# A row spread over the partitions by TensorE instead of by two transfers, once, in a Fourier mixing and feed-forward kernel

## The chip, the cores and the metric

The kernel runs on one core of a Trainium2 chip. The metric is the device time of one execution in microseconds. The engines are called as in the profile: PE (TensorE, with PEld for its weight loads), DVE (VectorE), ACT (ScalarE), POOL (GpSimd) and SP (SyncE, which here only issues transfers).

## The reference

For each of 8 batches of 3008 x 256 numbers, a Fourier transform runs along the sequence and then along the 256 features, and the real part is kept. Its 24064 rows then go through a feed-forward layer of 2048 inner features with the gate h * cos(h):

```python
X = np.fft.fft(x, axis=1)
X = np.fft.fft(X, axis=2)
x = X.real.reshape(24064, 256)
h = x @ w_in
g = h * np.cos(h)
out = g @ w_out
```

All of it is in 32-bit floats.

## The kernel before, in words

The transform along the sequence has two halves. `first_half` multiplies folded pieces of x by a small matrix (47 points), the result is rearranged by way of DRAM (`store_z`, `load_z`), and `second_half` multiplies by the 64-point part with the twiddle factors. The feature transform is folded into `w_in`, which gives two weight tiles `WC` and `WS`.

The outputs of one batch are worked through in 6 groups of columns (225 columns in group 0, 256 in the others). `second_half(b, g)` makes what a group needs: four pairs of matmuls into a borrowed PSUM bank `pb`, an ACT copy (L377) into the tile `pq`, and the tile `nb`. The second half of row 0 of `pq` holds the values of the Nyquist feature, and `nb` is this row repeated on all 128 partitions. For nearly all groups SP does that with two transfers, one of the row to a small DRAM tile `nd` (L383), and one back with a broadcast (L384). Only for the very first group, `spread_nb` does it otherwise: a matmul with a row of ones as weights (L391) writes the repeated row into a PSUM bank, and ACT copies it to `nb` (L392).

A group has 8 steps of two half-steps each; half-step k works on 128 of the 2048 inner features. The main loop runs over k (t is k // 2), and everything in it is written out by hand: the order of the program is the order on every engine, and nothing is planned by a scheduler. Several half-steps overlap. For one half-step the work is:

- ACT writes the seed, 0.25 plus a weight times `nb`, into a PSUM bank H (`seed`, L525). This is done one half-step ahead.
- PE adds the products with `WC` (`mm1(.., 0)`, L544), ACT keeps twice that in `ew` (`act_e`, L556), PE adds the products with `WS` (`mm1(.., 1)`, L544), and DVE writes the mirrored side (`dve_h`, L560).
- ACT rounds (L572), DVE takes the fraction (L576), ACT takes the sine (L582), and DVE forms the product with h (`dve_g`, L586), the last reader of the bank H.
- Once per step POOL forms sums of the products into a tile `S` (`sums`, L602, L608, L609), and PE multiplies seven blocks by combinations of `w_out` (`mm2`, L635), five half-steps behind (`LAG`).

The four H banks go round in turn. `borrow` gives the bank whose turn is next without moving the turn; what is written there must be read before the next seed writes it. At the end of each odd half-step come the combinations of finished groups, the stores of output (`store_out`), and the calls that the table `opening` names for step t (only in the first batch), then those that `transform` has set for the next batch: its loads of x (`load_x`, L147 to L155, on SP), its folds (`fold`, L241, on POOL), its halves of the transform. In step 4 the table calls `second_half(0, 1)`, and the calls for the next batch in the same step add `load_x(1, 2)`. Group 1 starts with half-step 16; its first seed is issued at the end of half-step 15. `combine_w2` in the same table forms combinations of `w_out` on POOL (L510) in steps 0 to 6.

```python
        4: ((combine_w2, 4, 6, 2, 4), (second_half, 0, 1)),
        5: ((combine_w2, 6, 8, 0, 2),),
```

SP takes its transfers strictly in the order of the program, and each is issued once its waits are over: the data, the room, and mostly the landing of the transfer issued eight before it, since eight semaphores go round.

Of the kernel before, what the change touches and what calls it, by code (L numbers as in the profile page):

```python
# [82 lines left out]
def _width(g):  # L83
    return 225 if g == 0 else 256
# [24 lines left out]
def kernel(  # L109
# [100 lines left out]
    def psum(name, tag="H"):  # L210
        at = tag
        if tag == "H":
            at = f"H{turn[0] % 4}"
            turn[0] += 1
        return ppool.tile([128, 512], FP, tag=at, bufs=bank[tag], name=name)

    def borrow(name, k=0):
        return ppool.tile([128, 512], FP, tag=f"H{(turn[0] + k) % 4}", bufs=1, name=name)
# [132 lines left out]
    ready = {}  # L351

    def second_half(b, g):

        T = _width(g)
        z2 = z2s[b]
        pb = borrow("pb") if b or g else psum("pb", "M")
        for q in range(4):
            jj = 4 * g + q
            nc.tensor.matmul(  # L360
                pb[:, 128 * q : 128 * q + 128],
                lhsT=z2[:, jj * 128 : jj * 128 + 128],
                rhs=BJ[:, jj * 128 : jj * 128 + 128],
                start=q == 0,
                stop=True,
                skip_group_check=True,
            )
        pq = spool.tile([128, 512], FP, tag="pq", bufs=8, name="pq")
        pv = pq[:, 0 : 2 * T].rearrange("d (e t) -> d e t", e=2)
        bv = pb.rearrange("d (q e k) -> d e q k", q=4, e=2)  # L370
        if g == 0:
            nc.scalar.copy(
                out=pv[:, :, 0:192].rearrange("d e (q k) -> d e q k", k=64), in_=bv[:, :, 1:4, :]
            )
            nc.scalar.copy(out=pv[:, :, 192:225], in_=bv[:, :, 0, 0:33])
        else:
            nc.scalar.copy(out=pv.rearrange("d e (q k) -> d e q k", k=64), in_=bv)  # L377
        nb = spool.tile([128, 256], FP, tag="nb", bufs=8, name="nb")
        ready[b, g] = (pq, nb)
        if b == 0 and g == 0:  # L380
            return
        nd = dpool.tile([1, 256], FP, tag="nd", bufs=4, name="nd")
        nc.sync.dma_start(out=nd[:, 0:T], in_=pq[0:1, T : 2 * T])  # L383
        nc.sync.dma_start(out=nb[:, 0:T], in_=nd[0:1, 0:T].to_broadcast([128, T]))  # L384


    def spread_nb():
        pq, nb = ready[0, 0]
        T = _width(0)
        pn = psum("pn", "M")  # L390
        nc.tensor.matmul(pn[:, 0:T], lhsT=ones, rhs=pq[0:1, T : 2 * T], start=True, stop=True)  # L391
        nc.scalar.copy(out=nb[:, 0:T], in_=pn[:, 0:T])  # L392

# [4 lines left out]
    def transform(b):  # L398
        todo = {}

        def at(o, *call):
            todo.setdefault(o, []).append(call)

        for p in range(4):
            at(2 * p, load_x, b, p)
            at(7 + p, take_middle, b, p)
            for k in range(4):
                at(8 * p + (6, 7, 9, 10)[k], fold, b, 2 * p + k // 2, k % 2)
            pairs[per * (b - 1) + 8 * p + 12] = b, 2 * p
            for c in (2 * p, 2 * p + 1):  # L410
                at(8 * p + 12, store_z, b, c)
        middles.add(per * (b - 1) + 11)
        at(23, load_z, b, 0)
        at(39, load_z, b, 1)
        for g in range(NG):
            at(42 + g, second_half, b, g)
        return todo
# [111 lines left out]
    def seed_first(h):  # L529
        s, T = h.s, h.s.T  # L530
        nc.tensor.matmul(
            h.H[:, 0:T],
            lhsT=wrow[:, 128 * h.u : 128 * h.u + 128],
            rhs=s.pq[0:1, T : 2 * T],
            start=False,
            stop=True,
            skip_group_check=True,
        )

    def mm1(h, e):  # L540
        s, T = h.s, h.s.T
        W = WS if e else WC
        f = 2 * s.fp + h.u
        nc.tensor.matmul(  # L544
            h.H[:, 0:T],
            lhsT=W[:, 128 * f : 128 * f + 128],
            rhs=s.pq[:, e * T : e * T + T],
            start=False,
            stop=True,
            skip_group_check=True,  # L550
        )

    def act_e(h):
        T = h.s.T
        h.ew = spool.tile([128, 256], FP, tag="ew", bufs=2, name="ew")
        nc.scalar.mul(out=h.ew[:, 0:T], in_=h.H[:, 0:T], mul=2.0)  # L556
# [27 lines left out]
    def dve_g(h):  # L584
        r, y = sides(h)
        nc.vector.scalar_tensor_tensor(  # L586
            out=r, in0=y, scalar=-0.25, in1=r, op0=ALU.add, op1=ALU.mult
        )
# [236 lines left out]
    for half in range(2):  # L825
# [5 lines left out]
        0: ((combine_w2, 0, 2), (combine_w2, 2, 4)),  # L831
        3: ((combine_w2, 4, 6, 0, 2),),
        4: ((combine_w2, 4, 6, 2, 4), (second_half, 0, 1)),
        5: ((combine_w2, 6, 8, 0, 2),),
        6: ((combine_w2, 6, 8, 2, 4),),
        10: ((second_half, 0, 2), (load_ident,)),
        14: ((second_half, 0, 3),),
# [12 lines left out]
    def step(t, last=None):  # L850
        s = steps[t] if 0 <= t < n else None
        return s if s is not None and (last is None or s.fp == 7) else None
# [3 lines left out]
    def unit(k):  # L856
        return halves[k] if 0 <= k < 2 * n else None
# [7 lines left out]
    for k in range(2 * n + LAG):  # L865
        t, u = divmod(k, 2)
        d, v = divmod(k - LAG, 2)
        cur, prev, old, nxt = unit(k), unit(k - 1), unit(k - 2), unit(k + 1)
        done = step(d)
        full = step(d if v else d - 1, True)  # L870
        if cur:
            if k % (2 * per) == 0:
                todo = transform(cur.s.b + 1) if cur.s.b + 1 < NB else {}
            if k >= AHEAD:
                mm1(cur, 0)
                act_e(cur)
            if k == 0:
                for h in (cur, nxt):
                    mm1(h, 0)
                    seed_first(h)  # L880
                    act_e(h)
                spread_nb()
            if k < AHEAD - 1:
                mm1(cur, 1)
            if k == 0:
                pw = [weights(1, 3)]
        pair = None if u else pairs.pop(t, None)
        if pair:
            b, c = pair
            pz = [first_half(b, c, borrow("pz"))]  # L890
        if old:
            dve_g(old)
            if old.u:
                sums(old.s)
        if pair:
            pz.append(first_half(b, c + 1, borrow("pz", 1)))
        pm = clear_middle() if u and t in middles else None
        if done:
            order = (0, 1, 5, 4, 3, 2, 6) if done is steps[-1] else range(7)
            mm2(done, 4 * v, 4 * v + 3, order)  # L900
        if pm is not None:
            middle(pm)
        if full and full is not steps[-1]:
            take_m(full, 1 if v else 3, nc.vector)
        if nxt and 0 < k < AHEAD - 1:
            seed(nxt)
        if prev:
            act_round(prev)
        if pm is not None:
            nc.scalar.copy(out=zm[64:128], in_=pm)  # L910
        if pair:
            keep_z(b, c, pz[0])
        if nxt and k >= AHEAD - 1:
            seed(nxt)
        if full and full is not steps[-1]:
            take_m(full, 0 if v else 2, nc.scalar)
        if prev:
            dve_frac(prev)
        if k + 1 in range(2, AHEAD):
            mm1(nxt, 0)  # L920
            act_e(nxt)
        if k == 1:
            pw.append(weights(0, 3))
        copy_small()
        if prev:
            act_sin(prev)
        if pair:
            keep_z(b, c + 1, pz[1])
            patch_z(b, c)
            patch_z(b, c + 1)  # L930
        if cur and k >= AHEAD - 1:
            mm1(cur, 1)
        if done and v == 0:
            mm2(done, 3, 4, order)
        if cur:
            dve_h(cur)
        if k in (1, 2):
            keep_weights(2 - k, 3, pw[k - 1], nc.vector.tensor_copy)
        elif k == 3:
            send_wn(3)  # L940
        elif k == 6:
            load_wn(3, nc.scalar)
        if u == 0:
            continue
        for i in range(6):
            s = step(t - 4 - i, True)
            if s:
                combine_m(s, i)
        for sg, lag in ((0, 8), (1, 10)):
            s = step(t - lag, True)  # L950
            if s:
                store_out(s, sg)
        for call in opening.pop(t, ()):
            call[0](*call[1:])
        for call in todo.pop(t % per, ()):
            call[0](*call[1:])
# [31 lines left out]
```

## Time and profile before

| | us |
|---|---|
| median of 3 runs | 1954.21 |
| lowest and highest run | 1953.16, 1957.72 |
| the profiled execution | 1952.79 |
| its span | 1951.0 |
| PE busy | 1935.9 (99%) |
| DVE, ACT, POOL busy | 1457.7, 1508.9, 1400.2 |
| mean granted clock of PE | 0.999 of full speed |

The span runs from the first to the last instruction that the profiler recorded, and the execution's own time has 1.8 us more around it. A matmul in 32-bit floats shows as two pieces of PE work. A line of the timeline gives the start, the time, the engine, the line of the kernel, the operation with its tiles, and in brackets how long the engine stood idle before it and on what. A line of the stretches gives, after the stretch and its length, for PE, PEld, DVE, ACT and POOL the busy time with the number of instructions, then the granted clock, the share of the transfer engines and the GB/s.

### The profile page before, as it was taken

The page shows a single profiled execution, that of the slowest core. Times are in us where ns is not written, and L with a number is a line of the kernel's source. Part 1 is how long each engine was busy: PE and PEld are TensorE (multiplying, and loading weights), DVE is VectorE, ACT ScalarE, POOL GpSimd, SP SyncE. Part 2 cuts the span into 40 slices and gives each one's busy share as a digit, 9 for nine tenths or more (in the row PEclk, how much of TensorE's full clock was granted, in tenths as well). Part 3 has the DMA queues.
Part 4 walks back from the last instruction along what each step waited for, and adds up shares of the span by engine and source line. Part 5 has one row for each costly group of instructions (what it writes and reads, how often), then busy time and mean ns, then how long its engine had stood idle before and what let it go on. Part 6 is the DMA issues. An engine that isn't in the chain of part 4 may idle for free.

```text
span 1951.0 us, 29624 instructions
## 1 busy us (share of the span) xinstructions
PE 1935.9 (99%) x9232; PEld 1682.9 (86%) x9232; DVE 1457.7 (75%) x2531; ACT 1508.9 (77%) x3444; POOL 1400.2 (72%) x1594
## 2 busy tenths in 40 slices
PE   8999999999999999999999999999999999999998
PEld 4888899888988889888898888988889888898887
DVE  3667777777777777777777777777777777778787
ACT  3777778777787777877778787787777887778775
POOL 3777767787677876787668776687767777666765
PEclk9999999999999999999999999999999999999999
DMA  7712024111230112301241111411124121110001
GB/s 184 141 27 44 20 47 84 24 36 33 53 71 18 40 40 59 54 20 40 43 78 31 32 34 41 86 24 39 24 42 84 24 40 28 39 22 16 11 14 31
DMA packets 178280, 88.71 MB, mean 45 GB/s; under 512 B 104890, under 2 KB 175209, under 8 KB 176492
## 3 DMA queue, kind: packets, MB, share of 16 engines
q1 hardware_dynamic: 176582, 86.35, 21.7%
q8 instruction: 75, 1.23, 0.3%
q14 instruction: 81, 0.66, 0.1%
q10 hardware_dynamic: 1542, 0.47, 0.1%
HBM read 49.51 MB, written 37.28 MB: 44 GB/s over the span
## 4 chain that ended last, share of the span: by engine, by line
PE 98%; DMA 1%; ACT 0%; DVE 0%; SPq 0%; issue 0%; POOL 0%; POOLq 0%; DVEq 0%
PE M L635 58%; PE H L544 33%; PE pz L269 3%; PE pb L360 2%; PE pw L427 1%; DMA xp<-in_x_dram 0%; DMA wr<-in_moe_w_in_dram 0%; DMA nb<-nd 0%; DMA nd<-pq 0%; PE pz L266 0%; PE pm L317 0%; DVE r L576 0%; DVE cb L703 0%; ACT r L582 0%; POOL xf L252 0%
## 5 line engine op out<-in xcount | busy, mean ns | idle before, releaser
L602 POOL TENSOR_TENSOR S<-r 128x512 f32<-128x512 f32 (+1 forms) x383 | 475.6, 1242 | 447.1 <-DVE r L586 398.5
L576 DVE SCALAR_TENSOR_TENSOR r<-r,H 128x512 f32<-128x512 f32 (+1 forms) x768 | 518.3, 675 | 195.5 <-ACT r L572 168.7
L582 ACT ACTIVATE r<-r 128x512 f32<-128x512 f32 (+1 forms) x768 | 477.0, 621 | 240.1 <-DVE r L576 235.2
L586 DVE SCALAR_TENSOR_TENSOR r<-H,r 128x512 f32<-128x512 f32 (+1 forms) x768 | 518.9, 676 | 133.8 <-ACT r L582 93.9
L635 PE MATMUL M<-S,VX 128*128 128x256 f32 (+1 forms) x2304 | 616.0, 376 | 0.0
L635 PEld LDWEIGHTS M<-S,VX 128*128 128x128 f32 x2304 | 436.0, 190 | 71.5 <-issue 22.7
L544 PE MATMUL H<-pq,WC 128*128 128x256 f32 (+1 forms) x1536 | 454.0, 377 | 3.9 <-ACT H L525 3.9
L544 PE MATMUL H<-pq,WS 128*128 128x256 f32 (+1 forms) x1536 | 451.1, 375 | 1.0 <-ACT ew L556 1.0
L572 ACT ACTIVATE r<-H 128x512 f32<-128x512 f32 (+1 forms) x768 | 447.7, 583 | 0.2 <-DVE H L560 0.2
L560 DVE TENSOR_TENSOR H<-ew,H 128x256 f32<-128x256 f32 (+1 forms) x768 | 324.7, 423 | 142.5 <-PE H L544 83.6
L635 PE MATMUL M<-r,w 128*128 128x256 f32 (+1 forms) x1536 | 387.6, 375 | 0.0
L556 ACT ACTIVATE ew<-H 128x256 f32<-128x256 f32 (+1 forms) x768 | 287.9, 375 | 121.5 <-PE H L544 117.0
L525 ACT ACTIVATE H<-nb,wn 128x256 f32<-128x256 f32 (+1 forms) x766 | 366.0, 478 | 4.9 <-DMA nb<-nd 4.0
L635 PEld LDWEIGHTS M<-r,w 128*128 128x128 f32 x1536 | 300.5, 196 | 26.9
L544 PEld LDWEIGHTS H<-pq,WC 128*128 128x128 f32 x1536 | 279.3, 190 | 48.3 <-ACT H L525 13.1
L544 PEld LDWEIGHTS H<-pq,WS 128*128 128x128 f32 x1536 | 290.0, 190 | 34.7 <-issue 1.6
L608 POOL TENSOR_TENSOR S<-S,r 128x256 f32<-128x256 f32 (+1 forms) x383 | 276.0, 721 | 30.0
L609 POOL TENSOR_TENSOR S<-r,S 128x256 f32<-128x256 f32 (+1 forms) x383 | 275.2, 718 | 30.0
L635 PE MATMUL M<-S,w 128*128 128x256 f32 (+1 forms) x768 | 225.5, 375 | 0.0
L635 PE MATMUL M<-r,VX 128*128 128x256 f32 (+1 forms) x768 | 225.2, 375 | 0.0
L635 PEld LDWEIGHTS M<-S,w 128*128 128x128 f32 x768 | 150.8, 197 | 14.6
L635 PEld LDWEIGHTS M<-r,VX 128*128 128x128 f32 x768 | 145.8, 190 | 14.6
(78 smaller groups left out, 918.1 us busy)
## 6 DMA issues: line engine op xcount, KB each, us to landing
out_dram<-ob SPq DMA_DIRECT2D x724, 32.0 KB
xp<-in_x_dram SPq DMA_DIRECT2D x56, 256.0 KB
zd<-zs SPq DMA_DIRECT2D x112, 96.0 KB
z<-zd SPq DMA_DIRECT2D x28, 384.0 KB
xp<-in_x_dram SPq DMA_DIRECT2D x56, 120.0 KB
nb<-nd SPq DMA_DIRECT2D x40, 128.0 KB
wr<-in_moe_w_in_dram SPq DMA_DIRECT2D x8, 256.0 KB
w<-in_moe_w_out_dram SPq DMA_DIRECT2D x4, 512.0 KB
```

What stands on the lines that cost most here:

```text
L525: nc.scalar.activation(out=h.H[:, 0:T], in_=s.nb[:, 0:T], func=AF.Copy, bias=0.25, scale=wn[:, f : f + 1])
L544: nc.tensor.matmul(h.H[:, 0:T], lhsT=W[:, 128 * f : 128 * f + 128], rhs=s.pq[:, e * T : e * T + T], start=False, stop=True, skip_group_che ...
L556: nc.scalar.mul(out=h.ew[:, 0:T], in_=h.H[:, 0:T], mul=2.0)
L560: nc.vector.tensor_tensor(out=h.H[:, T : 2 * T][:, ::-1], in0=h.ew[:, 0:T], in1=h.H[:, 0:T], op=ALU.subtract)
L572: nc.scalar.activation(out=r, in_=y, func=AF.Copy, bias=BIG, scale=1.0)
L576: nc.vector.scalar_tensor_tensor(out=r, in0=r, scalar=-BIG, in1=y, op0=ALU.add, op1=ALU.subtract)
L582: nc.scalar.activation(out=r, in_=r, func=AF.Sin, bias=0.0, scale=SIN_SCALE)
L586: nc.vector.scalar_tensor_tensor(out=r, in0=y, scalar=-0.25, in1=r, op0=ALU.add, op1=ALU.mult)
L602: tt(out=sv[:, 0:2], in0=qv[:, 1:2].to_broadcast([128, 2, T]), in1=qv[:, 0:4:3], op=ALU.subtract,)
L608: tt(out=sv[:, 2], in0=sv[:, 1], in1=gv[:, 0, 0], op=ALU.subtract)
L609: tt(out=sv[:, 3], in0=gv[:, 1, 0], in1=sv[:, 2], op=ALU.add)
L635: nc.tensor.matmul(acc[key][m // 2][:, 256 * (m % 2) : 256 * (m % 2) + T], lhsT=w, rhs=a, start=first, stop=s.fp == 7, skip_group_check=True,)
```

## The change

The row of group 1 of the first batch is spread in the same way as that of group 0. `second_half(0, 1)` stops before the two transfers. `spread_nb` takes the group as an argument, and for group 1 the matmul writes to a borrowed H bank instead of one of the banks for the outputs. It is called at the end of step 5, which is half-step 11, one step after `second_half(0, 1)`. All other spreads stay as they were.

```diff
-        if b == 0 and g == 0:
+        if b == 0 and g < 2:
             return
         nd = dpool.tile([1, 256], FP, tag="nd", bufs=4, name="nd")
         nc.sync.dma_start(out=nd[:, 0:T], in_=pq[0:1, T : 2 * T])
         nc.sync.dma_start(out=nb[:, 0:T], in_=nd[0:1, 0:T].to_broadcast([128, T]))
 
-    def spread_nb():
-        pq, nb = ready[0, 0]
-        T = _width(0)
-        pn = psum("pn", "M")
+    def spread_nb(g):
+        pq, nb = ready[0, g]
+        T = _width(g)
+        pn = borrow("pn") if g else psum("pn", "M")
         nc.tensor.matmul(pn[:, 0:T], lhsT=ones, rhs=pq[0:1, T : 2 * T], start=True, stop=True)
         nc.scalar.copy(out=nb[:, 0:T], in_=pn[:, 0:T])
...
-        5: ((combine_w2, 6, 8, 0, 2),),
+        5: ((combine_w2, 6, 8, 0, 2), (spread_nb, 1)),
...
-                spread_nb()
+                spread_nb(0)
```

## The prediction

> **What bounds the kernel now.** I read the page's busy times first, then the two-microsecond stretches around the place where PE pauses, then the list of waits, the timeline there, and SyncE's queue in the chain that ended last.
>
> Busy time by engine:
>
> ```profile
> PE 1935.9 (99%) x9232; PEld 1682.9 (86%) x9232; DVE 1457.7 (75%) x2531; ACT 1508.9 (77%) x3444; POOL 1400.2 (72%) x1594
> ```
>
> PE is idle for 15.1 us of 1951.0, so whatever the change gives must lie in those 15 us or in time when PE runs slowly. In the stretches after 82 us PE is busy in every microsecond up to 1930. The stretches in question (per engine the busy us, then granted clock, DMA share, GB/s):
>
> ```profile
> 70.00:72.00 2.00, 2.00 (x12) 1.89 (x10) 1.74 (x4) 1.22 (x3) 1.84 (x4) 1.00 0.13 37
> 72.00:74.00 2.00, 0.25 (x2) 0.00 (x0) 0.30 (x1) 0.00 (x0) 2.00 (x3) 1.00 0.65 113
> 74.00:76.00 2.00, 0.28 (x1) 0.28 (x2) 0.00 (x0) 0.81 (x2) 1.84 (x3) 0.86 1.08 182
> 76.00:78.00 2.00, 2.00 (x6) 1.71 (x7) 0.79 (x2) 1.19 (x4) 1.43 (x2) 0.50 1.12 181
> 78.00:80.00 2.00, 2.00 (x10) 1.82 (x9) 0.90 (x3) 0.98 (x5) 0.00 (x0) 0.79 1.01 137
> 80.00:82.00 2.00, 2.00 (x12) 1.92 (x11) 1.62 (x3) 1.61 (x4) 1.26 (x2) 1.00 1.07 120
> ```
>
> PE, DVE and ACT stand still from 72.25 to 75.2; then PE runs at a granted clock of 0.50 until about 78.9. The timeline names the cause:
>
> ```profile
> 71.33 0.54 PE L544 MATMUL H<-pq,WS 128*128 128x225 f32 x2
> 71.70 0.54 PE L635 MATMUL M<-S,VX 128*128 128x225 f32 x2
> ...
> 75.19 0.48 ACT L525 ACTIVATE H<-nb,wn 128x256 f32<-128x256 f32 x1 [3.97 <-DMA nb<-nd]
> ...
> 75.72 1.22 PE L544 MATMUL H<-pq,WC 128*128 128x256 f32 x2 [3.48 <-ACT H L525]
> ...
> 79.36 0.59 PE L544 MATMUL H<-pq,WC 128*128 128x256 f32 x2
> ...
> 81.74 0.59 PE L544 MATMUL H<-pq,WC 128*128 128x256 f32 x2
> ...
> 83.75 0.62 PE L544 MATMUL H<-pq,WC 128*128 128x256 f32 x2
> ```
>
> The seed of the first half-step of group 1 (half-step 16) needs nb of group 1. In SyncE's queue the copy to DRAM is issued at 68.11 and the copy back at 71.01:
>
> ```profile
> 67.55 0.41 SPq L155 DMA_DIRECT2D xp<-in_x_dram  x1
> 68.11 0.22 SPq L383 DMA_DIRECT2D nd<-pq  x1
> 71.01 0.36 SPq L384 DMA_DIRECT2D nb<-nd  x1
> 71.47 0.37 SPq L147 DMA_DIRECT2D xp<-in_x_dram  x1
> ```
>
> pq itself was written at 59.65 to 60.24. The chain that ended last gives the two transfers 2.89 and 4.16 us: nb lands at 75.17, and the seed starts at 75.19. So this round trip is on the path, once in the kernel.
>
> **The change, part by part.**
>
> *The wait that goes.* At 0.19 us a 225-column piece, the pair at 71.70 lets the next matmul start at 72.08. It starts at 75.72: 3.64 us. The half-step it opens then takes 75.72 to 79.36 = 3.64 us; the half-step of the same shapes two later takes 81.74 to 83.75 = 2.01 us. So 1.63 us are lost to the slow clock (from 75.72 to about 78.9 at half speed is 3.2 / 2 = 1.6, the same). Together 5.27 us.
>
> [...] The row: 0.86, 0.50 and 0.79 of three 2 us stretches make 0.28 + 1.00 + 0.42 = 1.70 us of clock lost, that is 3.4 us at half clock, after a pause of 3.5 us. [...]
>
> *Added on PE.* One matmul of a single row by 256 columns at the end of half-step 11, which in the trace of before is between the S,VX pair of 63.33 and the WC pair of 63.71. A pair of 256-column pieces takes 0.43 us start to start (78.92 to 79.36 is 0.44). Where single-row pieces stand between full ones, the starts are further apart: L544 at 36.80 to L531 at 37.38 is 0.58 instead of 0.38, and L391 at 37.86 to L544 at 38.33 is 0.47. Lower bound 0.43, upper 0.43 + 0.2 + 0.2 = 0.83; I take 0.7, nearer the rows that change from full to one row. PE is without a gap there (60 to 72 us), so all of it lands on the path. Its operands: pq has been there since 60.24; the borrowed bank was last read by the DVE product of half-step 9, at 62.23 to 62.85, 0.86 us before the matmul's turn. No wait on either.
>
> *Added on ACT.* One 128x256 copy out of the bank: the row for 128x225 is 0.35, for 128x512 (L377) 0.59, the 128x256 multiplication 0.38. I take 0.38. It stands behind the sine at 63.58 and ahead of the multiplication L556 at 64.29, which waits for WC of half-step 12. That WC is itself 0.7 later behind the new matmul, so the copy sits in the time ACT would wait: at 64.4 the pair for nb is done, copy to 64.8, WC done at 63.71 + 0.7 + 0.54 = 64.95. Cost on the path 0; if the cover is gone, at most 0.38. Queued behind the copy are the round and the seed of half-step 13 (64.97 to 65.43), which goes into this very bank; WC of 13 starts at 65.61, and both move by about the same 0.4 to 0.7.
>
> *Removed from SyncE.* Two issues (L383, L384), and the 3 us for which SyncE's queue stood at the second. Eight issues of x for batch 1 (71.47 to 75.19), of which the last started as nb landed, move up to about 68.1 to 71.5. Who needs them: the folds at 88.36 and 93.01 and the ACT copies at 88.37 and 93.59, none waiting for a transfer; they come 4.6 earlier, the loads about 3 earlier, and DMA is quiet (share 0.32 in 80 to 90). Gain or loss 0. The other 46 spreads keep their way and none makes ACT wait (only one wait on nb in the list).
>
> *What is late next.* POOL, which used the pause to catch up. It is busy 9.53 of 10 us from 60 to 70, and works without a gap to 77.43 (fold, sums of step 6 at 73.67 to 76.21, fold). Without the pause PE wants the first of these sums, ready at 74.73, by half-step 17's last S product, at 72.08 + 2.01 + 0.43 + 1.14 + 0.43 = 76.1, and the last, ready at 76.21, at about 77.7. Then step 7's sums run 77.43 to 80.0, wanted from 80.5. At least 1.4 us of slack everywhere, more with the new matmul in front. ACT: the seed of half-step 16 comes right after the round of 70.69, at 71.1 to 71.6, in time for 72.08. Cost 0.
>
> *Sum.* 5.27 - 0.7 = 4.6 us (4.4 to 4.8 by the bounds of the matmul alone). The profiled execution took 1952.79 us, span 1951.0 and 1.8 around it; it is 1.4 below the median 1954.21 of the runs. It would come to 1948.2, and I expect the median at 1954.21 - 4.6 = 1949.6.
>
> **The rivals.**
>
> *The slow clock is no part of the usual execution.* Then only 3.64 - 0.7 = 2.9 us are saved: 1951.3. [...] Against it: the runs are all above the profiled execution, while those without the slow clock should lie 1.6 below.
>
> *Another wait takes the place, on ACT.* ACT is busy 7.96 of 10 us in 60 to 70; if the copy and the longer chain behind it push the seeds 1 to 2 us out, PE pauses there and gets back part: gain 2.6 to 3.6, about 1951.2. For it: seeds already hold PE weight loads 43 times in the trace. Against it: 13.1 us in all, most of it this one pause, and the busy share leaves ACT 0.4 us in each half-step of 2.1 us.
>
> *Slower: POOL's sums of steps 6 and 7 come too late without the pause.* Place: the S products of half-steps 17 to 20. A PE pause of 3.0 us with the clock loss of 1.6 behind it uses up the 4.6; with the 1.4 us of slack, it decides from POOL 4.4 us late, which is almost a whole step's sums (2.5 us) and both folds (2.5 us) ahead of their need. A pause of 5 us would give 5 + 1.6 - 4.6 = 2.0 more than before, 1956.2. Against it: POOL's order doesn't change, and the folds found their x landed.
>
> *It doesn't do what it says.* In the changed build's order the two transfers are gone, and matmul and copy are there, so I give this nothing.
>
> **How the numbers follow.** A change under 0.2% (3.9 us) is about what a measurement of this kernel can't tell from none. Forecast 0.64; no slow clock usually 0.17; ACT 0.11; POOL 0.08. The forecast's own range is 1948.2 (the profiled execution's own) to 1950.6 (upper bound of the matmul, and the copy uncovered, with half a microsecond for the median); the two rivals of a smaller gain reach 1951.3, and the runs' median scatters by about 1. So 1947.6 to 1952.2 leaves out some 0.15. Faster by over 0.2%: the forecast and a little of the first rival that scatter carries over, 0.66; slower, POOL's case from 1958.1 on and scatter, 0.07; between 0.27.
>
> **What would show it.** In the changed kernel: one L391 of 256 columns near 63.7 and one L392 near 64.4, no L383 before about 88; no ACT wait on nb at all; PE busy 2.00 in each stretch from 60 to 82 and a clock of 1.00; the WC matmul of half-step 16 at about 72.8, that of 17 at about 74.8; the x issues done before 73; span about 1946.4. A PE wait on S or H between 72 and 82, or starts around L391 more than 0.9 apart, would make me wrong; so would a median that moves by 3 with a trace that moves by 4.6.

## The result, and the profile after

| | before | after |
|---|---|---|
| median of 12 runs, us | 1954.94 | 1949.2 |
| lowest and highest | 1952.75, 1959.14 | 1947.78, 1951.47 |
| the profiled execution | 1952.79 | 1951.47 |
| its span | 1951.0 | 1949.7 |

The ratio of after to before is 0.9968, with a 95% interval of 0.9959 to 0.9977: 4.5 to 8.0 us are saved, 5.7 between the medians. The forecast was 1949.6 and 4.6 us. The two profiled executions differ by only 1.3 us, though, so the traces have to be read with care.

The stretches of the changed kernel where PE stood still before (columns as before: the busy us of PE, PEld, DVE, ACT and POOL, then granted clock, transfer share, GB/s):

```profile
70.00:72.00 2.00, 2.00 (x13) 1.99 (x12) 1.75 (x4) 1.65 (x5) 1.29 (x2) 1.00 1.02 184
72.00:74.00 2.00, 2.00 (x12) 1.94 (x11) 1.44 (x3) 1.53 (x4) 1.84 (x4) 1.00 1.18 172
74.00:76.00 2.00, 2.00 (x13) 1.99 (x12) 1.67 (x5) 1.63 (x4) 1.92 (x3) 1.00 1.14 177
76.00:78.00 2.00, 2.00 (x12) 1.89 (x10) 1.36 (x3) 1.77 (x5) 1.92 (x3) 1.00 0.92 142
```

PE is never idle and its clock is 1.00. The timeline of the same kernel shows the new matmul, the copy, and the seed of half-step 16, which now waits for nothing:

```profile
66.60 0.54 PE L635 MATMUL M<-S,VX 128*128 128x225 f32 x2
67.07 0.69 PE L391 MATMUL pn<-pq,ones 1*128 1x256 f32 x2
67.70 0.65 PE L544 MATMUL H<-pq,WC 128*128 128x225 f32 x2
67.80 0.37 ACT L392 COPY nb<-pn 128x256 f32<-128x256 f32 x1
68.18 0.93 PE L635 MATMUL M<-S,VX 128*128 128x225 f32 x4
...
75.20 0.48 ACT L525 ACTIVATE H<-nb,wn 128x256 f32<-128x256 f32 x1
...
76.17 0.59 PE L544 MATMUL H<-pq,WC 128*128 128x256 f32 x2
...
78.18 0.59 PE L544 MATMUL H<-pq,WC 128*128 128x256 f32 x2
```

Half-step 16 takes 76.17 to 78.18 = 2.01 us, instead of 3.64. But it starts at 76.17, where before it could have started at 72.08. Of these 4.09 us, 0.82 are the new matmul: from the S,VX pair ahead of it to the S,VX four behind are 66.60 to 68.18 = 1.58 us, where two pairs alone take 0.76. The other 3.3 us were lost in the opening, whose program is the same in both kernels. Of these, 0.43 were lost ahead of 36 us (the first WC pair of 225 columns starts at 36.08, before at 35.65). These stretches of the changed kernel show where the rest went:

```profile
38.00:40.00 2.00, 2.00 (x8) 1.20 (x8) 0.40 (x1) 1.29 (x4) 1.78 (x3) 0.84 0.73 166
40.00:42.00 2.00, 2.00 (x4) 0.97 (x3) 0.62 (x1) 0.42 (x1) 0.25 (x1) 0.50 1.04 249
42.00:44.00 2.00, 2.00 (x7) 1.25 (x7) 0.76 (x2) 0.39 (x2) 1.92 (x4) 0.81 0.72 214
48.00:50.00 2.00, 1.23 (x4) 0.88 (x5) 1.49 (x4) 1.74 (x4) 1.84 (x3) 0.90 0.90 256
50.00:52.00 2.00, 2.00 (x6) 1.77 (x6) 1.53 (x4) 1.60 (x4) 0.20 (x1) 0.50 1.16 172
52.00:54.00 2.00, 2.00 (x9) 1.92 (x8) 1.11 (x3) 0.58 (x1) 1.29 (x2) 0.75 0.14 30
```

Two times PE ran at half clock; by the clock the losses are 0.32 + 1.00 + 0.38 and 0.20 + 1.00 + 0.50, together 3.4 us. By the starts of PE's work they put it back by 1.5 and 1.3 us, since in the second PE also stands idle for part of the time. In the first profile of before the clock is 1.00 in all of these. So the profiled execution of before was one of its best, that of after the slowest of its twelve. Which of it is chance the repeats had to show.

### The profile page after: what moved, and what is told of

Read it like the earlier page. It is cut to its first block, busy times and chain, and to the rows that moved or that the text cites. A ratio compares the mean times of both kernels' runs of the same rounds, so it can differ in the third digit from the quotient of the medians.

```text
span 1949.7 us, 29624 instructions
## 1 busy us (share of the span) xinstructions
PE 1936.4 (99%) x9234; PEld 1683.5 (86%) x9234; DVE 1458.3 (75%) x2531; ACT 1509.4 (77%) x3445; POOL 1399.8 (72%) x1594
## 4 chain that ended last, share of the span: by engine, by line
PE 98%; DMA 1%; DVE 0%; SPq 0%; ACT 0%; issue 0%; POOL 0%; POOLq 0%; DVEq 0%
PE M L635 59%; PE H L544 34%; PE pz L269 3%; PE pb L360 2%; DMA xp<-in_x_dram 1%; PE pw L427 1%; PE pz L266 0%; PE pm L317 0%; DVE cb L703 0%; SPq L147 0%; PE H L531 0%; PE po L733 0%; PE pn L391 0%; PE pd L491 0%; ACT H L525 0%
```

## The experiments

Theory A, formed after these two traces: PE's pause has no fixed length, since nb lands when SP's queue lets it; the change removes the whole of it, with the half clock behind it. Its rivals were a fixed pause (B), half clocks in the opening that the change itself brings (C), and a gain that comes from SP's freed queue.

**Both kernels once more** (no edit).

> The kernel before once more, for a second profile. Theory A (the pause has no fixed length: nb lands when SP's queue lets it, while PE arrives when its own work is done, so the pause and the half clock behind it differ between executions): the ACT wait for nb is not 3.97 us again but anywhere from 3 to 10 us, it goes with the moment at which SP issues nd (68.11 in the first profile), and the span goes with it. Theory B (pause 3.64 and clock 1.63 are fixed, 5.27 in all, and the median fell further than the trace foretold for another reason): the wait is again 3.5 to 4.5 us and the slow stretch 1.5 to 1.8.

> The changed kernel once more, for a second profile and more pairs of runs. Both theories: no ACT wait on nb, ratio about 0.997. Theory A: the two slow stretches of the first profile in the opening (at about 40 to 43 and 50 to 53 us, 3.4 us lost) are chance; in this profile their number or place differs, and the span with them by 1.7 per stretch (1946 to 1950). A third theory C, that the change brings these two stretches: they are there again, both, at the same places.

Before took 1957.8 us in the profiled execution, with a span of 1956.0. Its timeline, PE alone:

```profile
66.36 0.65 PE L544 MATMUL H<-pq,WC 128*128 128x225 f32 x2 [1.84 <-ACT H L525]
...
74.46 0.54 PE L635 MATMUL M<-S,VX 128*128 128x225 f32 x2
79.45 1.22 PE L544 MATMUL H<-pq,WC 128*128 128x256 f32 x2 [4.45 <-ACT H L525]
...
83.57 1.06 PE L544 MATMUL H<-pq,WC 128*128 128x256 f32 x2
...
86.73 0.59 PE L544 MATMUL H<-pq,WC 128*128 128x256 f32 x2
```

and SP's part of the same timeline:

```profile
54.54 0.36 SPq L147 DMA_DIRECT2D xp<-in_x_dram  x1
65.85 0.32 SPq L150 DMA_DIRECT2D xp<-in_x_dram  x1
...
69.96 0.22 SPq L383 DMA_DIRECT2D nd<-pq  x1
74.75 0.36 SPq L384 DMA_DIRECT2D nb<-nd  x1
```

PE could have gone on at 74.46 + 0.38 = 74.84 and did at 79.45: 4.61 us. Half-step 16 took 4.12 instead of 2.01, half-step 17 took 86.73 - 83.57 = 3.16 instead of 2.38: 2.89 us to the clock. That is 7.5 us, where the first profile had 5.27. nd was issued 1.9 us later and took 4.8 instead of 2.9 to land. B falls.

The two spans of before differ by 5.0 us, though, and these terms by 2.2 only. The other 2.8 PE had lost earlier (74.84 against 72.08), and 1.84 of it is the pause at 66.36: the seed of half-step 12 waited for wn, the weights that a seed multiplies nb by, whose last quarter comes by a transfer that ACT issues and that took 12.8 us to land here.

The changed kernel had a median of 1948.84 (ratio 0.9961, interval 0.9949 to 0.9974). In its second profile the opening's clock is 1.00 from 30 to 60 us, half-step 16 starts at 73.59, the span is 1947.0, and the new matmul costs 0.82 again. So C falls: the two slow stretches come and go with the execution. The second one, at about 50 us, left its mark also in two kernels below that lack the change: behind it ACT waits 1.04 us for PE in the first profile of the changed kernel (at 54.03), and it waits 1.06 us with the hop more (52.49) and 1.01 us with BJ later (51.84), where neither profile of before has such a wait from 50 to 56 us. The first was met in two kernels that have the change (the first profile of the changed kernel, and that without wn's transfers, with a clock of 0.92 from 35 to 40 us and 0.74 from 40 to 45), but at 38 to 44 us, ahead of anything that the change touches.

**The way through DRAM, but past SP's queue.**

```diff
+        if b == 0 and g == 1:
+            nc.scalar.dma_start(out=nd[:, 0:T], in_=pq[0:1, T : 2 * T])
+            later.append((nb, nd))
+            return
         nc.sync.dma_start(out=nd[:, 0:T], in_=pq[0:1, T : 2 * T])
...
+    later = []
+
+    def fetch_nb():
+        nb, nd = later.pop()
+        nc.scalar.dma_start(out=nb, in_=nd[0:1].to_broadcast([128, 256]))
...
-        5: ((combine_w2, 6, 8, 0, 2),),
+        5: ((combine_w2, 6, 8, 0, 2), (fetch_nb,)),
```

> The kernel before, but the two transfers of group 1 in the first batch are issued by ACT, the first right after the copy of pq and the second at the end of step 5; TensorE does nothing more. It separates the way through DRAM from the place in SP's queue. Theory A: nd is issued at about 60.5 and nb at 64 to 65, nb lands at 67 to 70, before half-step 16 needs it at 71; no wait on nb; the gain is that of the changed kernel or up to 0.7 more less 0.6 for ACT's issues: 4 to 8 us, ratio 0.996 to 0.998. The rival, that the way through DRAM is itself too long: nb lands after 72, PE still pauses, and the gain is under 2 us.

1948.83 us, ratio 0.9961 (0.9947 to 0.9975), the same as the changed kernel. ACT issues nd at 60.35 and nb at 64.12, the seed of half-step 16 runs at 71.60 and waits for nothing:

```profile
60.35 0.23 ACTq L384 DMA_DIRECT2D nd<-pq  x1
...
64.12 0.36 ACTq L394 DMA_DIRECT2D nb<-nd  x1
...
71.60 0.48 ACT L535 ACTIVATE H<-nb,wn 128x256 f32<-128x256 f32 x1
```

So the way through DRAM was not too long: its place behind SP's loads was. The 0.82 us of the matmul, which this kernel doesn't have, can't be seen between the two medians.

**The pause kept, PE kept working in it.**

```diff
+    def keep_warm(k):
+        pd = borrow("pd")
+        for i in range(k):
+            nc.tensor.matmul(
+                pd, lhsT=WC[:, 0:128], rhs=WC[:, 0:512], start=i == 0, stop=i == k - 1
+            )
...
+        7: ((keep_warm, 4),),
```

> The kernel before, with four matmuls of 512 columns whose result nobody reads, issued by PE right before half-step 16 (they write a borrowed bank and fill some 3.4 us of the pause). It separates the pause from the clock. If the half clock is the price of PE standing still: the granted clock stays at 1.00 after the pause, where the pause is no longer than 4 us; the ACT wait on nb stays as it is; the half-step of 16 takes 2.0 instead of 3.6 and the gain is 1.6 us (up to 0.5 less where the four end after nb). If the clock falls for another reason, the slow stretch stays and the time is the same or longer by 0.5.

1952.16 us, ratio 0.9986 (0.9976 to 0.9996): 0.8 to 4.7 us less than before, and 3 us more than the changed kernel. Between the medians of these runs lie 3.7 us, more than the 1.6 that were expected. Its timeline (L502 are the four matmuls, L551 is the H matmul here) and the stretch that had the clock of 0.50 before:

```profile
72.44 3.60 PE L502 MATMUL pd<-WC 128*128 128x512 f32 x8
75.98 0.70 PE L551 MATMUL H<-pq,WC 128*128 128x256 f32 x2
...
78.09 0.59 PE L551 MATMUL H<-pq,WC 128*128 128x256 f32 x2
```

```profile
76.00:78.00 2.00, 2.00 (x11) 1.84 (x11) 1.06 (x2) 1.71 (x6) 1.92 (x3) 1.00 1.12 170
```

ACT still waited 3.9 us for nb, and half-step 16 started 75.98 - 72.44 = 3.54 late, but then it took 2.11 instead of 3.64. So here the slow stretch (a clock of 0.50 from 76 to 78 us in the first profile of before, 1.00 in this one) is the price of PE standing still, and 5.27 splits into pause and clock as the prediction had it. The granted clocks of the single executions bear out the 3.7: their mean is 0.9972 in the fifteen of before that were run alongside and 0.9991 in these eleven, and 0.0019 of 1950 us is 3.7 us.

**The changed kernel, with SP's two transfers kept**, to a tile that nobody reads.

```diff
-        if b == 0 and g < 2:
+        if b == 0 and g == 0:
             return
+        if b == 0 and g == 1:
+            nb = cpool.tile([128, 256], FP, tag="nbx", name="nbx")
         nd = dpool.tile([1, 256], FP, tag="nd", bufs=4, name="nd")
```

> The changed kernel, but SP still issues the two transfers of group 1 where it did, to a tile that nobody reads. It separates the wait of ACT from what SP's queue gains by losing two issues and the 3 to 5 us it stood at the second. Theory A: only the wait counted; the x loads are 3 us later again, still hidden, and the time is that of the changed kernel, ratio 0.995 to 0.998, no gap of PE at half-step 16. The rival, that the freed queue gave part of the gain: PE or ACT waits for x or for another transfer between 75 and 100 us, and the ratio is nearer 1 by 1 us or more (0.998 and up).

1948.95 us, ratio 0.9971 (0.9962 to 0.9981). SP issues the two at 67.73 and 70.63, within 0.4 us of the first profile of before, and PE goes on at 72.96:

```profile
67.73 0.22 SPq L385 DMA_DIRECT2D nd<-pq  x1
...
70.63 0.36 SPq L386 DMA_DIRECT2D nbx<-nd  x1
```

```profile
72.96 0.59 PE L546 MATMUL H<-pq,WC 128*128 128x256 f32 x2
```

Only the wait counted; the freed queue gave nothing. This trace is also the fair partner of the first one of before, since its opening ran alike: PE could start half-step 16 at 72.96 against 72.08, 0.88 later, which is the matmul's 0.82 and little else, and the spans are 1946.5 and 1951.0. That is 4.5, and 5.27 - 0.82 is 4.45.

**One hop more in the way.**

```diff
         nc.sync.dma_start(out=nd[:, 0:T], in_=pq[0:1, T : 2 * T])
+        if b == 0 and g == 1:
+            ne = dpool.tile([1, 256], FP, tag="ne", bufs=1, name="ne")
+            nc.sync.dma_start(out=ne, in_=nd)
+            nd = ne
```

> The kernel before with one more transfer in the way of group 1 in the first batch: nd is copied to a second DRAM tile, from which nb is read. It lengthens the wait by one hop, 2 to 5 us, with no work on TensorE. Theory A: every microsecond of it is on the path; the pause grows from 3.5 to 4.5 to 6 to 9 us, the half clock behind it stays for one to two stretches of 3.4 us, and the kernel is 2 to 5 us slower than before, ratio 1.001 to 1.003. The rival, that the wait was hidden in part: less than 1 us slower.

1957.66 us, ratio 1.0019 (1.0008 to 1.003). In its trace PE's pause is 7.04 us:

```profile
81.60 1.22 PE L548 MATMUL H<-pq,WC 128*128 128x256 f32 x2 [7.04 <-ACT H L529]
```

and half-step 16 behind it takes 4.07 us. SP issues the hop at 74.88 and the load of nb at 76.79, so it costs 1.9 us in this trace, and the medians are 2.8 apart (1.6 to 5.9 by the interval). So the hop is on the path, and nothing covers it.

**The matmul eight times, and seven of the eight with full rows.**

```diff
-        nc.tensor.matmul(pn[:, 0:T], lhsT=ones, rhs=pq[0:1, T : 2 * T], start=True, stop=True)
+        for _ in range(8 if g else 1):
+            nc.tensor.matmul(
+                pn[:, 0:T], lhsT=ones, rhs=pq[0:1, T : 2 * T], start=True, stop=True
+            )
```

```diff
+        for _ in range(7 if g else 0):
+            nc.tensor.matmul(
+                pn[:, 0:T], lhsT=WC[:, 0:128], rhs=pq[:, T : 2 * T], start=True, stop=True
+            )
         nc.tensor.matmul(pn[:, 0:T], lhsT=ones, rhs=pq[0:1, T : 2 * T], start=True, stop=True)
```

> The changed kernel with its spreading matmul issued eight times in a row to the same place. It prices the matmul alone. The first two profiles of the changed kernel give 0.82 us for one (from the S,VX pair ahead to the S,VX four behind: 1.58 instead of 0.76), of which 0.43 is streaming; seven more should add 7 x 0.43 = 3.0 us if the rest is the change to a single row and back, once, or 7 x 0.6 = 4.2 if every single-row pair costs the 0.57 to 0.62 that the rows show. So the time is 1952 to 1953.5, and PE has no gap at half-step 16.

> The run with the spreading matmul eight times, but seven of the eight have full weights and a full moving tile (128 rows) instead of one row; as many columns. It separates the work from the clock: in the run with eight single rows PE had no gap and its clock still fell to half for 3.4 us right behind them. If rows that stand still count as idleness for the clock: the clock stays 1.00 from 60 to 80, and the eight cost 8 x 0.43 + 0.4 = 3.8 instead of 3.6 + 1.7 = 5.3, so 1952 us, 2 to 3 us under that run. If the clock falls for another reason: the slow stretch is there again and the time is the same as in that run, 1954 to 1955.

Eight single rows: 1954.78 us, ratio 0.9999 (0.9988 to 1.0011); all of the gain is gone, and the time is above the 1952 to 1953.5 that were expected. Seven full and one single: 1952.03, ratio 0.998 (0.9972 to 0.9989). The timelines, first of the eight single rows, then of the full ones:

```profile
64.27 0.54 PE L638 MATMUL M<-S,VX 128*128 128x225 f32 x2
64.75 3.71 PE L392 MATMUL pn<-pq,ones 1*128 1x256 f32 x16
68.39 0.65 PE L547 MATMUL H<-pq,WC 128*128 128x225 f32 x2
68.88 1.36 PE L638 MATMUL M<-S,VX 128*128 128x225 f32 x4
```

```profile
63.44 3.19 PE L392 MATMUL pn<-pq,WC 128*128 128x256 f32 x14
66.56 0.69 PE L395 MATMUL pn<-pq,ones 1*128 1x256 f32 x2
67.18 0.65 PE L548 MATMUL H<-pq,WC 128*128 128x225 f32 x2
```

The eight take 68.39 - 64.75 = 3.64 us here and 67.18 - 63.44 = 3.74 there, for the same number of columns. The clock is not the same. The stretches of the eight single rows and then of the full ones:

```profile
65.00:70.00 5.00, 5.00 (x22) 4.16 (x22) 0.72 (x2) 2.25 (x6) 3.67 (x5) 0.92 0.65 138
70.00:75.00 5.00, 5.00 (x21) 4.70 (x20) 2.85 (x6) 2.56 (x7) 2.00 (x3) 0.74 1.07 174
```

```profile
65.00:70.00 5.00, 5.00 (x25) 4.15 (x24) 1.06 (x3) 2.16 (x6) 3.26 (x5) 1.00 1.08 205
70.00:75.00 5.00, 5.00 (x28) 4.93 (x27) 4.05 (x8) 4.13 (x11) 4.03 (x6) 1.00 1.04 212
```

With single rows, PE's busy share is 5.00 of 5 and yet 5 x 0.08 + 5 x 0.26 = 1.7 us go to the clock; with full rows nothing does. The medians differ by 2.7. The mean granted clocks of the single executions, 0.9979 over ten and 0.9993 over eleven, differ by as much: 0.0014 of 1952 us is 2.7 us. For the price of one matmul, the same reckoning as above gives 3.85 us for the eight (from the S,VX pair at 64.27 to the S,VX four at 68.88, less 0.76) where one costs 0.82. So seven more cost 3.03, or 0.43 each, which is what a pair of 256 columns with 128 rows takes too (73.59 to 74.03 is 0.44 in the second profile of the changed kernel), and the change to a single row and back takes the other 0.39, once.

**What holds SP's queue.** Two edits of before, and one of them in the changed kernel too. The last 1 MB load of BJ goes behind the two transfers:

```diff
-    load_bj(1024, NJ * 128)
...
-        5: ((combine_w2, 6, 8, 0, 2),),
+        5: ((combine_w2, 6, 8, 0, 2), (load_bj, 1024, NJ * 128)),
```

> The kernel before with nothing changed but the issue of the last 1 MB load of BJ (columns from 1024), which moves from before the first x load of batch 1 to the end of step 5, behind the two transfers of group 1. TensorE does nothing more and the way through DRAM stays with SP. If what stands ahead in SP's queue, by its size and by the wait for the landing eight issues back, makes nb late: nd is issued at 61 to 65 instead of 68 to 70, nb lands before 72 or little after, and the gain is 4 to 8 us as in the run with ACT's queue. If it is the loads of x that hold the queue: nd is still at 67 or later and the gain is under 2 us.

1950.28 us, ratio 0.9978 (0.9966 to 0.9989). nd was not issued earlier (67.81), so the way in which this was meant to work is refuted. Its trace doesn't explain the gain. nb was issued at 71.55 and landed just before the x load at 75.73, issued eight behind it, later than in the first profile of before (71.01 and 75.17), and the pause is short because PE came later, behind the slow stretch of the opening that ACT's wait at 51.84 marks: it could have gone on at 73.16, there at 72.08. This execution took 1951.88, above the median; what the edit saves in the others stays open. PE in this trace:

```profile
76.27 0.70 PE L544 MATMUL H<-pq,WC 128*128 128x256 f32 x2 [2.95 <-ACT H L525]
...
78.38 0.60 PE L544 MATMUL H<-pq,WC 128*128 128x256 f32 x2
```

After 2.95 us of idleness the clock was 1.00 from 60 to 95 us, and half-step 16 took 2.11.

In every trace up to here SP stood at an x load, for 4.3 to 10.9 us, until ACT's transfer wn<-wd had landed, with which that load has no data in common. The waits of SP's queue in the second profile of before, 50 to 70 us, show 10.9 us of it (4.3 in the first). In the trace just above it is 7.9 us: SP goes on at 63.41, and from there its issues follow one right behind the other to nd at 67.81. Theory D: this transfer holds nd.

```diff
-    def weight_row(n):
+    def weight_row(n, pw=None):
         row = WS[0:1, 512 * n : 512 * n + 512]
-        pw = psum("pw", "M")
+        pw = pw or psum("pw", "M")
...
         elif k == 3:
-            send_wn(3)
-        elif k == 6:
-            load_wn(3, nc.scalar)
+            keep_wn(3, weight_row(3, borrow("pw")))
```

> The kernel before, with the weights' column wn of the fourth quarter made by four one-column matmuls and an ACT copy of 4 columns at half-step 3, instead of by two transfers through DRAM that ACT issues; the spread of group 1 stays with SP. In every trace so far SP stands 4.3 to 10.9 us between 55 and 67, at an x load whose semaphore was last used by ACT's transfer wn<-wd. Theory D (that transfer holds SP's queue, and so nd and nb): nd is issued at 60 to 63, right after pq, nb lands before 72, no pause, gain 5 to 7 us, ratio 0.996 to 0.998. The rival, that the wait only moves to the next landing of eight back (x or BJ): nd still at 66 or later and a gain under 2 us.

> The same edit in the changed kernel. Theory D: the pause is gone already, so the gain over the changed kernel is only what ACT waited for wn at half-step 12 in some executions (0.75 us in the first profile of the changed kernel, nothing in the second), less some 0.3 us of small matmuls: the same time within 1 us, 1948 to 1949.5, and no run much above 1950.

These two kernels don't compute the whole function: the small matmuls begin the borrowed bank anew, and by the argument, not by a run, half-step 5 loses its seed by it. Its instructions all run, so the times stand. In before: 1951.87, ratio 0.9983 (0.9974 to 0.9992), and SP's timeline:

```profile
55.71 0.35 SPq L147 DMA_DIRECT2D xp<-in_x_dram  x1
56.10 0.42 SPq L150 DMA_DIRECT2D xp<-in_x_dram  x1
...
61.59 0.32 SPq L147 DMA_DIRECT2D xp<-in_x_dram  x1
66.94 0.33 SPq L155 DMA_DIRECT2D xp<-in_x_dram  x1
68.59 0.33 SPq L147 DMA_DIRECT2D xp<-in_x_dram  x1
69.01 0.37 SPq L155 DMA_DIRECT2D xp<-in_x_dram  x1
69.88 0.22 SPq L383 DMA_DIRECT2D nd<-pq  x1
71.58 0.36 SPq L384 DMA_DIRECT2D nb<-nd  x1
```

SP goes on at 56 instead of 59 to 66, but then it stands for 5.0 us ahead of the x load at 66.94 (the same load waits 3.0 us for BJ to land in the first profile of before) and for 1.3 and 0.5 us more up to nd, which is issued at 69.88 all the same; PE pauses for 3.60 us. So D is not the whole cause: in this execution the loads ahead hold the queue without wn. But it took 1953.44, above the median. Five of the eleven took 1950.2 to 1951.5 with a granted clock of 1.000, less than 1 us of clock lost, which leaves no room for a slow stretch of 1.6. The transfer counts, since the kernel is 1.6 to 5.1 us faster than before; whether by way of nd or of the seed of half-step 12, which waits for wn itself (1.84 us of PE in the second profile of before), was not tried. By which of them the pause is longest in an execution stays open.

In the changed kernel the edit gave 1949.96, ratio 0.9969 (0.9958 to 0.998), no gain over the changed kernel's 1948.84 to 1949.2, and a little above the 1948 to 1949.5 that were expected. With wn's transfers gone from both kernels, the change is worth 1951.87 - 1949.96 = 1.9 us between the medians, where with them it was 5.7. The intervals of the two ratios overlap, so this hints at a good part for that transfer in the usual pause and doesn't size it. No run was better than the changed kernel beyond the intervals.

## Why the prediction was right, and where its size was off

- *The wait on nb is on the path and goes.* Right. The matmul, ACT's queue and the kept transfers each end it or leave it as foretold, and the hop more shows from the other side that it was not covered.
- *The pause and the half clock, 3.64 + 1.63 = 5.27.* Right for that execution, and the clock term was shown by itself: 3.64 to 2.11 for half-step 16 with PE kept working. As the size for the usual execution it is too small, and this is the term of the sum that was mis-sized: the second profile measures 4.61 + 2.89 = 7.5. Less the matmul's 0.82, the two make 4.45 and 6.7, and the difference of the medians, 5.7, lies between. The clock's part alone, estimated from the mean granted clocks of fifteen executions of before and five of the changed kernel run alongside (0.9972 and 0.9988), is 0.0016 of 1950 us, some 3 us where the prediction had 1.63. The profiled execution had been read as 1.4 below the median; against the median of twelve it is 2.2 below, and the other trace of before, with the longer pause, is that of an execution of 1957.8.
- *The forecast of 1949.6.* That it lies 0.4 from the measured 1949.2 is in part luck: the median of before came out 0.7 above the three runs that it started from, and the gain 1.1 above the 4.6, and the two nearly cancel.
- *The rival that the usual execution has no half clock.* It didn't happen: of five traces with a pause ahead of half-step 16, the four of 3.48, 3.60, 4.45 and 7.04 us had it, and only that of 2.95 had none. Its chance of 0.17 was the author's estimate. In the trace with 3.60 the clock fell only when PE was at work again: from the WC pair at 76.41 to the next start are 0.53 us, as in the trace with 2.95 (0.54), but the four pieces of S,VX at 76.94 take 1.32 to the next start, where that trace has 0.76.
- *The matmul, 0.7 between 0.43 and 0.83.* It measured 0.82 in both profiles of the changed kernel. The upper bound was the right one: 0.43 for its 256 columns and 0.39 for the change to a single row and back. In the second profile these 0.39 are 0.09 ahead of the matmul, 0.19 behind it and 0.11 behind the WC pair that follows.
- *ACT's copy at nothing.* Right. It took 0.37 us, stood in ACT's wait for the matmul, and no PE wait on a seed followed. One reading against the rival on ACT was wrong: of the 13.1 us that weight loads waited for seeds in before, this pause is 3.83, not most. In the first profile of the changed kernel it is 9.1 us, so the rest stayed as it was, and the rival didn't happen.
- *SP's queue at nothing, POOL's slack.* Right. The run with the kept transfers gives the same time, and no PE wait on S stands in the lists of the changed kernel.
- *The foretold places* (matmul near 63.7, half-step 16 at 72.8) hold for the trace with the kept transfers (63.86 and 72.96) and not for the first profile of the changed kernel (67.07 and 76.17), which met the two slow stretches in the opening; in the second they are 64.49 and 73.59. The x issues were not done before 73 but at 73.92 in the second profile and 77.14 in the first; between 60 and 100 us no compute engine waited for an x load in the first, and neither PE nor ACT in the second.

## What to carry to other kernels

The wait on the same transfer was 3.97 us in one trace of before and 4.9 in the other. So before the price of a wait is taken from a trace, ask what sets its two ends, here the landing behind other loads and the arrival of PE, and look at a second execution. Look at what stands ahead of a small transfer in its queue: nd went out at 68.11 and 69.96 behind SP's loads, and at 60.35 by ACT's queue. Another queue did as well here as another way of moving the data (1948.83 and 1948.84 us). A pause of PE of some 3.5 us cost half as much again through the clock in two traces here (1.70 us of clock each, behind pauses of 3.48 and 3.60).

## What the runs showed that was not expected

The granted clock fell in a stretch where PE was busy in every microsecond: sixteen single-row pieces of 256 columns in a row (3.64 us) were followed by half clock for about 3.4 us (0.92 from 65 to 70 us and 0.74 from 70 to 75), while the same number of columns with 128 rows in all but the last matmul left the clock at 1.00. One such matmul alone, as the change has it, showed no fall in four traces. The single-row matmuls of the opening (36.6 to 38.8 us) are followed by the half clock at 39 in the first profile of the changed kernel and in that of the changed kernel without wn's transfers; that they are its cause was not tried, and in seven other traces (both of before, the second of the changed kernel, those of ACT's queue and of the pause kept, before without wn's transfers, and the full rows) the clock is 1.00 from 35 to 45 us. The slow stretch at about 50 us came without a long pause: ahead of it PE has only four gaps of 0.16 to 0.54 us, which stand in the first profile of before too, where the clock stayed at 1.00. The slow stretches of these traces whose clock is given here lost 1.7 us each to it, which is 3.4 us at half clock, and those behind the pauses of 4.45 and 7.04 us lost 3.4, twice that (by a clock of 0.58, 0.50, 0.50 and 0.71 in the four stretches from 78 to 86 us in the one, and of 0.88, 0.50 and 0.94 in the three from 75 to 90 in the other).
